# Eight single halves: another division of the weight splitting over ScalarE, VectorE and GpSimd in the expert stage

## The chip, the cores and the metric

One core of a Trainium2 chip. The metric is the device time of one execution in microseconds (us).

## The reference, cut to what matters

Linear attention, then a dense feed-forward layer (384 to 2048 to 384), then a mixture of 8 experts with one expert for each of the 1536 tokens. The change lies in the expert stage alone:

```
for e in range(8):                         # disp[e]: the tokens sent to expert e
    h[e] = maximum(disp[e] @ w1[e], 0)     # w1[e]: 384 x 1024
    y[e] = h[e] @ w2[e]                    # w2[e]: 1024 x 384
out[token] = gate_w[token] * y[expert of the token]
```

All of it is float32.

## The kernel before, in words

The attention and the dense layer take the first 300 us or so. In between, tokens are routed: their rows are scattered to a table in memory (`disp`), a region for each expert, and `counts` says how many there are. Then the experts run one after the other.

**Float32 in three products.** TensorE multiplies in a shorter format (`fp32r`). So each operand is split in a high part (a cast of the number) and a low part (the number less its high part), and high x high, high x low and low x high are summed. The weights of an expert are split on the chip too: four pieces `q` (two halves of `w1`, two of `w2`), each in two halves `x` of 128x768 numbers. `split_expert` (L667) does one half: a cast (L674 on ScalarE, L676 on VectorE), then a subtraction (L677). That makes eight casts and eight subtractions for each expert.

**One block.** `expert_block` (L758) computes 128 tokens of one expert. On TensorE: `hidden(0)` (nine matmuls, L775), five matmuls of `hidden(1)`, four transposes of the first half of the hidden layer (L784), the last four matmuls of `hidden(1)`, transposes of the next expert's rows (L658), three quarters of the first products with `w2` (L799), the second transposes, and the rest of the products. ScalarE does the two relus (L779) and the two casts of the transposed hidden layer (`hh`, L789); VectorE makes its low parts (`hl`, L790), and the result times the gate weight (`y`, L683). GpSimd scatters `y` to the output by an indirect DMA (L684, "put").

**Work beside a block.** `also(n)` (L765) stands at five places of a block and issues what the dictionary `beside` (L835 to L839) holds for it. In an expert's first block this is the splitting for the next expert. Before: place 0 (behind the matmuls of `hidden(0)`, ahead of the first relu): piece 0, cast and subtraction on VectorE. Place 1 (ahead of the first `hh`): piece 1, cast on ScalarE, subtraction on GpSimd. Place 2: transposes of the next expert's rows. Place 3 (behind the second relu, ahead of the second `hh`): piece 2, as piece 1. Place 4: the rows' own split (`d`, L663 and L664), then piece 3, cast on ScalarE, subtraction on VectorE. Each engine works in the order in which its instructions are issued.

**More blocks.** Up to three blocks, the second and third under a condition on the number of tokens (L846). With these inputs experts 0 to 3 have two blocks, expert 4 three, experts 5, 6 and 7 one (part of expert 0 was done earlier). Every engine reads the count itself (L1123) and branches.

**Loads.** SP's queue issues them in order. `load_expert(e + 2)` fetches the raw weights of the expert after the next (L392, L395), and waits until the same buffers' last splitting (expert e) is done. `load_rows(e)` (L639, its DMA on L644) fetches an expert's rows; there are three buffers, so the rows of e + 3 wait for the last put of expert e. Before, the loop at L1117 issues `load_rows(e + 3)` behind expert e, and so ahead of `load_expert(e + 3)`.

Of the kernel before, what the change touches and what calls it, by code (L numbers as in the profile page):

```python
# [23 lines left out]
def kernel(  # L24
# [16 lines left out]
    nc = tc.nc  # L41
# [4 lines left out]
    E = w_gate.shape[1]  # L46
# [337 lines left out]
    def load_expert(e, q):  # L384
        if q % 2 == 0:
            if e % 2 == 0:
                raws[("e", e)] = wpool.tile([P, 2 * PIECE], F32, tag="w", name=f"re{e}_{q}")
            else:
                raws[("e", e)] = late["p"].tile([P, 2 * PIECE], F32, tag=f"lraw{q}", name=f"re{e}_{q}")
        t = raws[("e", e)][:, (q % 2) * PIECE:(q % 2 + 1) * PIECE]  # L390
        if q < 2:
            nc.sync.dma_start(t.rearrange("p (c f) -> p c f", c=DC),  # L392
                              w1[e, :, q * HF:(q + 1) * HF].rearrange("(c p) f -> p c f", p=P))
        else:
            nc.sync.dma_start(t.rearrange("p (c d) -> p c d", d=DM),  # L395
                              w2[e, (q - 2) * HF:(q - 1) * HF, :].rearrange("(c p) d -> p c d", p=P))
        raws[("e", e, q)] = t
# [238 lines left out]
    def region(e):  # L636
        return (E - 1 - e) * STRIDE

    def load_rows(e):  # L639
        pool, tag = ((p1, "rows"), (late["p"], "lrows"), (late["p"], "erows"))[e % 3]  # L640
        t = pool.tile([P, SB, ROW], F32, tag=tag, name=f"drow{e}")
        base = region(e) + (P if e == 0 else 0)
        for b0, b1 in ((0, 1), (1, 2), (2, SB)) if e == 0 else ((0, SB),):
            nc.sync.dma_start(t[:, b0:b1], disp[base + b0 * P:base + b1 * P, :].rearrange("(b p) d -> p b d", p=P))  # L644
        dsp[e] = t

    def claim(e):

        dT[e] = [p2.tile([P, DC, STRIDE], F32R, tag=("xh", "xl")[x], name=f"d{x}_{e}") for x in range(2)]
        for q in range(NPIECE):  # L650
            wsl[("e", e, q)] = wpool.tile([P, 2 * PIECE], F32R, tag="w", name=f"we{e}_{q}")

    def prep(e, b):

        t = dsp[e]
        pt = bank(f"pd{e}_{b}", "acc")
        for c in range(DC):
            nc.tensor.transpose(pt[:, c * P:(c + 1) * P], t[:, b, c * P:(c + 1) * P], ident)  # L658
        src = pt[:, 0:DM].rearrange("p (c t) -> p c t", c=DC)
        hi = dT[e][0][:, :, b * P:(b + 1) * P]  # L660

        def g():
            nc.scalar.copy(hi, src)  # L663
            nc.vector.tensor_tensor(dT[e][1][:, :, b * P:(b + 1) * P], src, hi.bitcast(F32), ALU.subtract)  # L664
        return g

    def split_expert(e, q, x, he, le):  # L667
        src = raws[("e", e, q)]
        t = wsl[("e", e, q)]
        h = PIECE // 2  # L670
        sl = slice(x * h, (x + 1) * h)
        sl2 = slice(PIECE + x * h, PIECE + (x + 1) * h)
        if he is nc.scalar:
            nc.scalar.copy(t[:, sl], src[:, sl])  # L674
        else:
            he.tensor_copy(t[:, sl], src[:, sl])  # L676
        le.tensor_tensor(t[:, sl2], src[:, sl], t[:, sl].bitcast(F32), ALU.subtract)  # L677
# [147 lines left out]
    def expert(e, val):  # L825

        beside = {}
        if e + 1 < E:
            got = []

            def split(q, he, le):
                for x in range(2):
                    split_expert(e + 1, q, x, he, le)

            beside = {0: [lambda: split(0, nc.vector, nc.vector)],  # L835
                      1: [lambda: split(1, nc.scalar, nc.gpsimd)],
                      2: [lambda: got.extend(prep(e + 1, b) for b in range(2))],
                      3: [lambda: split(2, nc.scalar, nc.gpsimd)],
                      4: [lambda: [g() for g in got], lambda: split(3, nc.scalar, nc.vector)]}  # L839
        if e == 0:  # L840
            for g in [prep(0, b) for b in range(2)]:
                g()
        expert_block(e, 0, beside)

        def more(b):
            with tc.If(val > b * P):  # L846
                got = []
                expert_block(e, b, {2: [lambda: got.append(prep(e, b + 1))], 4: [lambda: got[0]()]} if b + 1 < SB else {})
                if b + 1 < SB:
                    more(b + 1)  # L850
        more(1)


    with tc.manual_schedule():
# [140 lines left out]
        for q in range(NW):  # L995
            for x in range(2):
# [9 lines left out]
                for n, p in enumerate(CONVERT.get(at, OTHERS)):  # L1006
                    g = at + p // 5
# [3 lines left out]
        for i in range(FRONT, NTILE):  # L1011
            blk = max(x for x in range(NBLK) if FIRST[x] <= i)
            sub = i - FIRST[blk]
            for f, then, at in PHASES:
                g = (blk - 1) * NFT + at[sub]
# [50 lines left out]
        g, n = NBLK * NFT - 1, SIZES[-1]  # L1066
# [50 lines left out]
        for e in range(E):  # L1117
            if e + 1 < E:
                claim(e + 1)
            if e + 2 < E:  # L1120
                for q in range(NPIECE):
                    load_expert(e + 2, q)
            val = nc.values_load(counts[0:1, e:e + 1], min_val=0, max_val=NT)  # L1123
            if e == 0:
                load_rows(2)
            expert(e, val)
            if e + 3 < E:
                load_rows(e + 3)


# [28 lines left out]
```

## Time and profile before

| | us |
|---|---|
| median of 3 runs | 471.08 (470.81 to 471.49) |
| the profiled execution | 470.56 |
| its span, first to last instruction | 468.8 |
| TensorE matmul busy | 437.5 (93%) |
| TensorE weight load busy | 383.7 (82%) |
| VectorE busy | 287.4 (61%) |
| ScalarE busy | 196.3 (42%) |
| GpSimd busy | 170.4 (36%) |

All times below are us from the start of the span. PE is TensorE, PEld its weight load, DVE VectorE, ACT ScalarE, POOL GpSimd, SP the queue that issues the loads; a q behind an engine's name is its sequencer. A line of a timeline has start, duration, engine, line of the kernel, operation, output<-input, the number of tokens of the matmul or the shape, the count, and in brackets the idle time just before it and what ended it. A line of windows has the stretch, its length, the busy time of PE, PEld, DVE, ACT and POOL with the number of their instructions, the clock granted to TensorE as a share of the full one, the DMA engines' busy share and the GB/s that they moved. The expert stage runs from about 316 to the end.

### The profile page before, as it was taken

The numbers are of one execution on the slowest core, as the hardware profiler recorded it, in microseconds if no ns is written. First come the engines' busy times: TensorE is split into PE (matmuls) and PEld (weight loads), VectorE is DVE, ScalarE is ACT, GpSimd is POOL, SyncE is SP. The second block draws the span as 40 slices with busy tenths as digits, with TensorE's granted clock in tenths as the row PEclk, the third lists the DMA queues.
The fourth block names the chain that finished last, engine by engine and source line by source line (L and its number), as shares of the span: only waits on it lengthen the run. The fifth ranks groups of instructions, "written<-read, shape, count | busy, mean of one in ns | idle before, by whom it ended". The sixth has DMA issues, their size and how long they took to land. (4 is left out here: it accounts for less than half of the span.)

```text
span 468.8 us, 7834 instructions
## 1 busy us (share of the span) xinstructions
PE 437.5 (93%) x3039; PEld 383.7 (82%) x3039; DVE 287.4 (61%) x477; ACT 196.3 (42%) x330; POOL 170.4 (36%) x145
## 2 busy tenths in 40 slices
PE   7977989699899999999999999999999999999975
PEld 6765778488788898989988889988888988888864
DVE  6898998999744354436334764346564556644771
ACT  1336644444444333323434444327264553624731
POOL 6845457464240232101200120036262543622760
PEclk9998999989999999999999999999999999999988
DMA  7999950559510208002600020039281835630900
GB/s 136 219 258 262 332 146 18 168 168 367 158 35 1 51 1 279 9 0 107 233 0 1 5 81 0 1 102 330 97 308 52 315 131 211 230 126 25 323 18 9
DMA packets 70603, 62.28 MB, mean 133 GB/s; under 512 B 41934, under 2 KB 58238, under 8 KB 70560
## 3 DMA queue, kind: packets, MB, share of 16 engines
q1 hardware_dynamic: 68832, 57.29, 39.8%
q0 software_dynamic: 1728, 4.40, 2.5%
q8 instruction: 28, 0.46, 0.4%
q14 instruction: 15, 0.12, 0.1%
HBM read 49.99 MB, written 12.62 MB: 134 GB/s over the span
## 5 line engine op out<-in xcount | busy, mean ns | idle before, releaser
L584 PE MATMUL acc<-wm,gh 128*128 128x384 f32 x384 | 100.9, 343 | 0.5 <-POOL wm L368 0.5
L599 PE MATMUL h<-xh,wm 128*128 128x512 f32 (+1 forms) x294 | 87.0, 405 | 3.8 <-DVE gl L622 3.8
L618 DVE SCALAR_TENSOR_TENSOR h<-ng,sign,h 128x512 f32<-128x512 f32 x48 | 36.1, 752 | 67.9 <-ACT ng L615 67.9
L584 PEld LDWEIGHTS acc<-wm,gh 128*128 128x128 f32 x384 | 68.8, 188 | 4.9 <-POOL wm L368 1.1
L775 PE MATMUL eh<-we,d 128*128 128x512 f32 x252 | 65.1, 403 | 4.3 <-PEq L846 4.3
L584 PE MATMUL acc<-wm,gl 128*128 128x384 f32 x192 | 64.9, 338 | 0.0
L599 PEld LDWEIGHTS h<-xh,wm 128*128 128x128 f32 x294 | 53.0, 191 | 13.4 <-issue 2.9
L677 POOL TENSOR_TENSOR we<-re,we 128x768 fp32r<-128x768 f32 x28 | 54.0, 1959 | 16.3 <-ACT we L674 16.2
L775 PEld LDWEIGHTS eh<-we,d 128*128 128x128 f32 x252 | 45.7, 188 | 15.1 <-issue 5.1
L615 ACT ACTIVATE ng<-h,slope 128x512 f32<-128x512 f32 x48 | 33.0, 688 | 57.0 <-PE h L599 57.0
L619 ACT CAST gh<-h 128x512 fp32r<-128x512 f32 x48 | 28.1, 586 | 63.7 <-DVE h L618 63.7
L799 PE MATMUL ey<-we,hh 128*128 128x384 f32 x224 | 49.0, 352 | 0.0
L522 POOL DMA_INDIRECT disp<-rows,sl x12 | 12.6, 1052 | 99.9 <-DVE run L543 64.4
L368 POOL TENSOR_TENSOR wm<-rm,wm 128x768 fp32r<-128x768 f32 x16 | 31.5, 1966 | 47.6 <-ACT wm L367 43.8
L790 DVE TENSOR_TENSOR hl<-pht,hh 128x512 fp32r<-128x512 f32 x28 | 19.3, 691 | 47.0 <-ACT hh L789 45.2
L677 DVE TENSOR_TENSOR we<-re,we 128x768 fp32r<-128x768 f32 x36 | 46.8, 1316 | 1.0 <-ACT we L674 0.3
L599 PE MATMUL h<-xl,wm 128*128 128x512 f32 (+1 forms) x147 | 42.9, 401 | 0.7 <-DVE xl L270 0.7
L622 DVE TENSOR_TENSOR gl<-h,gh 128x512 fp32r<-128x512 f32 x48 | 33.0, 687 | 15.6 <-ACT gh L619 15.6
L779 ACT ACTIVATE hs<-eh 128x512 f32<-128x512 f32 x28 | 16.8, 600 | 58.6 <-PE eh L775 58.6
L674 ACT CAST we<-re 128x768 fp32r<-128x768 f32 x50 | 39.6, 839 | 0.0
L799 PEld LDWEIGHTS ey<-we,hh 128*128 128x128 f32 x224 | 38.9, 193 | 0.4 <-ACT hh L789 0.4
L684 POOL DMA_INDIRECT out_dram<-y,drow x14 | 14.5, 1035 | 63.7 <-DVEq L846 38.6
(182 smaller groups left out, 659.2 us busy)
## 6 DMA issues: line engine op xcount, KB each, us to landing
re<-in_moe_w_dram SPq DMA_DIRECT2D x32, 768.0 KB, 8.5
rm<-in_moe_w_in_dram SPq DMA_DIRECT2D x8, 768.0 KB, 8.2
rm<-in_moe_w_out_dram SPq DMA_DIRECT2D x8, 768.0 KB, 6.6
disp<-rowss SPq DMA_DIRECT2D x1, 4825.0 KB, 17.3
drow<-disp SPq DMA_DIRECT2D x7, 579.0 KB, 4.2
out_dram<-rowss SPq DMA_DIRECT2D x1, 2304.0 KB, 22.6
kn<-in_k_dram SPq DMA_DIRECT2D x10, 192.0 KB, 4.4
rn<-in_r_dram SPq DMA_DIRECT2D x10, 192.0 KB, 4.8
```

What stands on the lines that cost most here:

```text
L368: eng.tensor_tensor(lo, low.bitcast(F32), hi.bitcast(F32), ALU.subtract)
L584: nc.tensor.matmul(accs[(blk, s)], gs[g][a][:, s * P:(s + 1) * P], wout[b][:, ft % 2, :], start=(ft == 0 and n == 0), stop=(ft == NFT - 1 ...
L599: nc.tensor.matmul(phs[g][:, cols[0]:cols[1]], win[a][:, c, o:o + P], xs[b][:, c, cols[0]:cols[1]], start=(n == 0), stop=(n == 3 * DC - 1))
L615: nc.scalar.activation(ng, ph, AF.Relu, scale=slope[:, ft:ft + 1])
L618: nc.vector.scalar_tensor_tensor(ph, ng, sign[:, ft:ft + 1], ph, op0=ALU.mult, op1=ALU.add)
L619: nc.scalar.copy(gh, ph)
L622: nc.vector.tensor_tensor(gl, ph, gh.bitcast(F32), ALU.subtract)
L674: nc.scalar.copy(t[:, sl], src[:, sl])
L677: le.tensor_tensor(t[:, sl2], src[:, sl], t[:, sl].bitcast(F32), ALU.subtract)
L775: nc.tensor.matmul(ph[q], d[x][:, c, :], ww[y][:, c, :], start=(n == 0), stop=(n == 3 * DC - 1))
L790: nc.vector.tensor_tensor(hl, pt, hh.bitcast(F32), ALU.subtract)
L799: nc.tensor.matmul(py, hT[q][x][:, c * P:(c + 1) * P], ww[y][:, c, :], start=(q == 0 and not low and c == 0 and y == 0), stop=(q == 1 and ...
```

## The change

Where the eight halves of the splitting stand in a block, and on which engine. All eight casts are on ScalarE. Subtractions: five on VectorE (V), three on GpSimd (G). And `load_rows(e + 2)` moves behind `load_expert(e + 2)`, ahead of expert e.

```
-            def split(q, he, le):
-                for x in range(2):
-                    split_expert(e + 1, q, x, he, le)
-
-            beside = {0: [lambda: split(0, nc.vector, nc.vector)],
-                      1: [lambda: split(1, nc.scalar, nc.gpsimd)],
+            def split(*what):
+
+                return [lambda q=q, x=x, le=le: split_expert(e + 1, q, x, nc.scalar, le) for q, x, le in what]
+
+            V, G = nc.vector, nc.gpsimd
+            beside = {0: split((0, 0, V), (0, 1, V)),
+                      1: split((1, 0, G)),
                       2: [lambda: got.extend(prep(e + 1, b) for b in range(2))],
-                      3: [lambda: split(2, nc.scalar, nc.gpsimd)],
-                      4: [lambda: [g() for g in got], lambda: split(3, nc.scalar, nc.vector)]}
+                      3: split((1, 1, V), (2, 0, G)),
+                      4: [lambda: [g() for g in got], *split((2, 1, V), (3, 0, V), (3, 1, G))]}
...
             if e + 2 < E:
                 for q in range(NPIECE):
                     load_expert(e + 2, q)
+                load_rows(e + 2)
             val = nc.values_load(counts[0:1, e:e + 1], min_val=0, max_val=NT)
-            if e == 0:
-                load_rows(2)
             expert(e, val)
-            if e + 3 < E:
-                load_rows(e + 3)
```

## Rows read from the trace of the kernel before

**Rows 1.** Windows by expert: 1, 5, 6 (columns: end of the profile section above).

```profile
337.50:358.00 20.50, 19.72 (x109) 17.55 (x109) 12.01 (x15) 10.15 (x17) 9.25 (x6) 1.00 0.58 203
...
428.00:438.20 10.20, 10.17 (x58) 8.88 (x56) 6.72 (x10) 7.41 (x12) 7.53 (x5) 1.00 0.55 189
438.20:453.50 15.30, 11.98 (x56) 10.42 (x56) 14.38 (x14) 7.41 (x12) 10.86 (x6) 0.89 0.40 141
```

**Rows 2.** Timeline of TensorE, experts 5, 6 and the start of 7.

```profile
428.07 3.44 PE L775 MATMUL eh<-we,d 128*128 128x512 f32 x14
431.35 0.60 PE L784 MATMUL pht<-ident,hs 128*128 128x128 f32 x4
...
435.92 1.55 PE L799 MATMUL ey<-we,hh 128*128 128x384 f32 x8
...
438.72 3.51 PE L775 MATMUL eh<-we,d 128*128 128x512 f32 x14 [0.55 <-PEq L846]
...
448.83 1.65 PE L799 MATMUL ey<-we,hl 128*128 128x384 f32 x4 [2.73 <-DVE hl L790]
...
453.98 3.51 PE L775 MATMUL eh<-we,d 128*128 128x512 f32 x14 [0.55 <-PEq L846]
```

**Rows 3.** Windows inside expert 6: TensorE's wait, and the stretch behind it (columns as rows 1).

```profile
445.90:448.80 2.90, 0.20 (x2) 0.00 (x0) 2.90 (x3) 2.73 (x5) 2.90 (x2) 1.00 0.01 3
448.80:452.30 3.50, 3.47 (x11) 3.48 (x12) 3.50 (x4) 0.00 (x0) 2.84 (x2) 0.51 0.02 5
```

**Rows 4.** Timeline of VectorE, experts 5 and 6.

```profile
428.92 0.56 DVE L676 CAST we<-re 128x768 fp32r<-128x768 f32 x1
429.52 0.96 DVE L677 TENSOR_TENSOR we<-re,we 128x768 fp32r<-128x768 f32 x1
...
437.29 3.48 DVE L677 TENSOR_TENSOR we<-re,we 128x768 fp32r<-128x768 f32 x2
440.69 0.61 DVE L683 TENSOR_SCALAR y<-ey,drow 128x384 f32<-128x384 f32 x1
442.01 0.56 DVE L676 CAST we<-re 128x768 fp32r<-128x768 f32 x1 [0.72 <-DMA re<-in_moe_w_dram]
...
443.48 2.20 DVE L676 CAST we<-re 128x768 fp32r<-128x768 f32 x1
445.72 2.45 DVE L677 TENSOR_TENSOR we<-re,we 128x768 fp32r<-128x768 f32 x1
448.09 1.28 DVE L790 TENSOR_TENSOR hl<-pht,hh 128x512 fp32r<-128x512 f32 x2
```

**Rows 5.** Timeline of GpSimd, experts 4 to 6.

```profile
403.27 7.97 POOL L677 TENSOR_TENSOR we<-re,we 128x768 fp32r<-128x768 f32 x4 [3.01 <-ACT we L674]
...
429.17 1.16 POOL L684 DMA_INDIRECT out_dram<-y,drow  x1 [8.29 <-DVE y L683]
431.83 7.24 POOL L677 TENSOR_TENSOR we<-re,we 128x768 fp32r<-128x768 f32 x4 [1.50 <-ACT we L674]
...
442.78 8.86 POOL L677 TENSOR_TENSOR we<-re,we 128x768 fp32r<-128x768 f32 x4
```

**Rows 6.** Timeline of SP's queue: rows and weights of expert 7.

```profile
432.09 0.37 SPq L644 DMA_DIRECT2D drow<-disp  x1
432.55 0.97 SPq L392 DMA_DIRECT2D re<-in_moe_w_dram  x2
```

**Rows 7.** The page's DMA issues: line, engine, count, KB each, us to landing.

```profile
re<-in_moe_w_dram SPq DMA_DIRECT2D x32, 768.0 KB, 8.5
```

**Rows 8.** Timeline of ScalarE, expert 5.

```profile
430.43 0.60 ACT L779 ACTIVATE hs<-eh 128x512 f32<-128x512 f32 x1 [4.71 <-PE eh L775]
...
435.12 0.59 ACT L789 CAST hh<-pht 128x512 fp32r<-128x512 f32 x1
...
436.34 1.59 ACT L674 CAST we<-re 128x768 fp32r<-128x768 f32 x2
```

**Rows 9.** Groups by line, 316 to 454: ScalarE's casts, busy and mean ns.

```profile
L674 ACT CAST we<-re 128x768 fp32r<-128x768 f32 x42 | 33.0, 840 | 0.0
```

## The prediction

> **What bounds the kernel now.** I read the windows by expert first, to see in which experts TensorE is not full. In expert 1 it is busy 19.72 of 20.50 us, and the missing 0.78 us is one gap at an expert's start, which the timeline puts down to TensorE's own sequencer at the branch; expert 5 is full, 10.17 of 10.20; expert 6 is not, 11.98 of 15.30 [rows 1]. Experts 0 and 2 to 4 look like expert 1. So in seven of eight experts nothing that the other engines do is on the path, and faster splitting is worth nothing there. Expert 6 is where time can be had: both have one block, yet from start to start expert 5 takes 438.72 - 428.07 = 10.65 us and expert 6 453.98 - 438.72 = 15.26 us, which is 4.61 us more [rows 2].
>
> Next the timeline of TensorE in expert 6: one wait of 2.73 us, ended by VectorE's `hl` [rows 2]. Behind it the granted clock is 0.51 for some 3.5 us, the lower of the two levels (1.2 against 2.4 GHz); ahead of it and in the wait it was 1.00 [rows 3]. Half speed for 3.5 us is some 1.75 us more, and 2.73 + 1.75 = 4.48, nearly all of the 4.61.
>
> Why `hl` was late stands in VectorE's and GpSimd's timelines [rows 4, 5]. Four things follow on one another. (1) In expert 5, VectorE's last two subtractions take 3.48 us where one alone takes 0.96: they meet GpSimd's run of four, which ends at 431.83 + 7.24 = 439.07. (2) So `y` of expert 5, queued behind, comes at 440.69, though TensorE began expert 6 at 438.72. (3) VectorE's first cast of expert 6 starts at 442.01, the last 0.72 us waiting for expert 7's weights: those loads were issued from 432.55, behind the rows [rows 6]; landing takes a median of 8.5 us [rows 7]. (4) Then the second cast takes 2.20 us and the subtraction 2.45 us, beside GpSimd's run from 442.78. `hl` is queued behind all that, at 448.09.
>
> **The change, part by part.**
>
> *Casts of piece 0, from VectorE to ScalarE.* VectorE loses two casts of 0.56 us an expert [rows 4], ScalarE gains two of 0.84 [rows 9]. They now stand ahead of the first relu in ScalarE's queue, and behind that relu wait TensorE's transposes. ScalarE is idle 4.71 us before that relu [rows 8], so two casts (some 1.6 us) have room. In expert 5 the relu starts at 430.43, ends at 431.03, and the transposes come at 431.35 [rows 2, 8]: 0.32 us to spare. The casts are late only if they start after 430.43 + 0.32 - 1.59 = 429.16, that is 1.09 us after TensorE's first matmul. How soon ScalarE may start, no row shows; VectorE's cast into the same buffer started at 428.92, 0.85 us after it, and not before its own `y` was done [rows 4]. Bounds: no delay, or, should ScalarE start as late as VectorE did in expert 6 (3.29 us after the first matmul), 2.2 us. I take none, as the cast of expert 5 is the nearest row, and ScalarE has no `y` to do first.
>
> *Piece 1.* One cast instead of two ahead of the first `hh`, so `hh` and `hl` come up to 0.5 us sooner: nothing on the path. The other half moves to place 3, in a pair of casts ahead of the second `hh`, as many as before, so that `hh` still ends at 435.12 + 0.59 = 435.71, 0.21 us before the products that need it [rows 2, 8]. Zero, with a small margin.
>
> *Place 4.* ScalarE does three casts instead of two. Two ended at 436.34 + 1.59 = 437.93 [rows 8]; a third ends at about 438.7. TensorE started expert 6 at 438.72, so a one-block expert just holds it; should TensorE's next bank wait for ScalarE's branch, 0 to 0.2 us at each of two starts (experts 6 and 7). I take 0.1 for both together. After that ScalarE branches, casts piece 0 of expert 7 from about 439.3 to 440.9, and the relu of expert 6 is due at 438.72 + 2.36 = 441.1. It fits.
>
> *Subtractions.* GpSimd has three instead of four: 3 x 1.81 = 5.4 us of 10.65 instead of 7.2 [rows 5]. They are apart now: in expert 5 after the casts at about 431.8, 435.1 and 438.7, with gaps between. VectorE has five instead of four and no casts: 5 x 0.96 = 4.8 against 2 x 0.56 + 4 x 0.96 = 5.0 us without meetings. I place VectorE's in those gaps: half (1,1) at 434.3 to 435.3; the last two at 437.3 to 439.2, when GpSimd is idle. `y` of expert 5 then starts at about 439.2 instead of 440.69. In expert 6, `hl` of the first half comes at about 443.3 and of the second at about 446.4; TensorE wants the first at about 445.9 (where it began to wait before [rows 3]). It wants the second behind eight products that in expert 5 end at 435.92 + 1.55 = 437.47, 9.40 us after its start [rows 2], so at about 448.1. Both are early. So the wait of 2.73 us goes, and with it the fall of the clock: 4.61 us off.
>
> A meeting still costs: the row of 3.48 us against 2 x 0.96 says up to 1.6 us on VectorE each time. The Trainium skill (SBUF — State Buffer, "SBUF: two separate sides") says that a VectorE operation with two SBUF inputs and a GpSimd operation exclude each other for a whole instruction. By that rule five subtractions on VectorE can be held up where only four could before; the rows agree that a meeting costs nearly a whole GpSimd instruction (1.6 against 1.81), which gives a rival below.
>
> *Loads.* The weights of e + 2 no longer stand behind rows that wait for the put of e - 1. For expert 7 the rows' wait ended at 432.09, 2.9 us after expert 4's last put at 429.17 [rows 5, 6]. What is left to wait for is the splitting of expert 5, in expert 4's first block, whose GpSimd part ended at 403.27 + 7.97 = 411.24 [rows 5]. So the loads go at about 412, land some 8 to 10 us later, and the wait of 0.72 us goes; it lies inside the chain above, so no further gain. The rows of expert 7 go at 432 as before and are wanted at 443: nothing. SP issues no instruction more. Where two blocks follow, the loads were early enough and nothing changes.
>
> **Sum.** The profiled execution took 470.56 with a span of 468.8. 470.56 - 4.61 + 0.1 = 466.05. The median shown is 0.52 above that execution; on it the forecast is 466.6 us.
>
> **Rivals.**
>
> *Meetings remain* (GpSimd and VectorE subtract at the same time, and `hl` of the second half is late). If GpSimd's first half starts 0.4 us later in expert 6, VectorE's half (1,1) waits a whole 1.81 us, ends near 447.8, and `hl` near 448.5, 0.5 us late. In expert 6 alone that leaves 467.1; in all seven first blocks 7 x 0.5 = 3.5, which is 470.1. For it: the third subtraction on GpSimd comes at the very end of a one-block expert. Against: 1.0 to 1.5 us of room in expert 5. Chance 0.10, likely at 467 to 469.
>
> *The weights are late all the same* (SP is held by something that the rows do not show). Then ScalarE's cast in expert 6 waits until 442.0, the relu behind it starts at 443.6 and ends at 444.2, and TensorE waits 2.1 us for its transposes; with a clock fall of 1.75 that is 3.9 of the 4.6 given back: 470.4. Against: the only long wait ahead of these loads is that of the rows. Chance 0.04. This would also be how "the change does nothing" looks.
>
> *ScalarE late at every first relu* (slower). If whatever frees the buffers lets the casts start only 3.29 us after the first matmul, as in expert 6 before, each of seven first blocks loses 2.2 us: 466.6 + 15.4 = 482.0. It decides from 1.09 us on; the time is above the old one by 0.2% when the casts start on average about 1.9 us after. For it: ScalarE gets the slower casts, and one late cast now blocks relus. Against: 4.71 us of idle time before the relu, and VectorE's start at 0.85. In a sentence of its own: the Trainium skill (ScalarE: Activation LUTs, "Rules for kernel authors") advises VectorE for simple elementwise work, and its 186 ns + 0.833 ns an element makes 826 ns for such a cast, an estimate that the 840 ns here agree with [rows 9]. By that rule, were every ScalarE cast on the path, 14 of them at 0.84 - 0.56 = 0.28 us dearer would take 3.9 us of the gain. Chance of this rival 0.04.
>
> **How the numbers follow.** Forecast 0.82, meetings 0.10, late weights 0.04, ScalarE late 0.04. About 0.2%, 0.9 us, is what a measurement can tell. Faster: the forecast, most of the meetings, 0.91; the same: the late weights and the far end of the meetings, 0.05; slower 0.04. The range: below, the forecast less 0.8 us (no 0.1 us at the starts and the spread of the runs, 0.4 us, with a little more gained from `y` coming earlier); above, up to the middle of the meetings, 2 us: 465.8 to 468.6.
>
> **What would show it.** Expert 6 takes 10.6 to 10.8 us from start to start, like expert 5; no wait for `hl`; granted clock 1.00 through all experts; `y` of expert 5 near 439.2; expert 7's weight loads near 412; first relu still 2.3 to 2.5 us after an expert's first matmul. It would be wrong if the windows showed TensorE below 19.7 us in a two-block expert, or a wait on the first relu anywhere.

## The result, and the profile after

The changed kernel takes 466.36 us (median of 6 runs, 465.58 to 467.54), the kernel before, measured beside it, 470.94: a ratio of 0.9908, 95% interval 0.9892 to 0.9925, so 0.75% to 1.1% faster. The forecast was 466.6, range 465.8 to 468.6. The profiled execution took 466.23 with a span of 464.5; the forecast for it was 466.05. The kernels of the later rounds below that come out like the change are 3.6 to 4.1 us under the kernel before measured beside them, so the 4.5 us here are a figure of this round and of the two traces.

The windows by expert, after (columns as [rows 1]; expert 1, expert 5, expert 6):

```profile
337.60:358.10 20.50, 19.72 (x109) 17.55 (x109) 9.83 (x14) 11.78 (x20) 7.75 (x5) 1.00 0.66 221
428.00:438.20 10.20, 10.20 (x58) 8.95 (x56) 6.49 (x9) 6.98 (x12) 5.35 (x3) 1.00 0.24 80
438.20:448.90 10.70, 10.11 (x57) 8.91 (x56) 7.74 (x11) 9.01 (x15) 7.38 (x4) 1.00 0.04 13
```

Expert 1 has the same 19.72 busy us of TensorE as in [rows 1], to the hundredth, although VectorE does 2.2 us less beside it and ScalarE 1.6 more: there the splitting was not on the path. Expert 6 has a granted clock of 1.00 instead of 0.89, and TensorE is busy 10.11 of 10.70 us.

The timeline of TensorE after: starts of experts 5, 6 and 7, and the products in expert 6 that had waited for `hl` in [rows 2]:

```profile
428.14 3.44 PE L775 MATMUL eh<-we,d 128*128 128x512 f32 x14
...
438.83 3.54 PE L775 MATMUL eh<-we,d 128*128 128x512 f32 x14 [0.59 <-ACTq L847]
...
446.07 0.86 PE L799 MATMUL ey<-we,hl 128*128 128x384 f32 x4
...
449.61 3.54 PE L775 MATMUL eh<-we,d 128*128 128x512 f32 x14 [0.59 <-ACTq L847]
```

From start to start expert 5 takes 10.69 us (10.65 before), expert 6 takes 449.61 - 438.83 = 10.78 (15.26 before). The 4.48 us less in expert 6 are all of the gain between the two traces: the spans differ by 4.3, and the rest is tenths (expert 5 starts 0.07 later than before, and from expert 7's start to the end it is 14.9 instead of 14.8). The wait and the slow products are gone; the gap at an expert's start is 0.59 instead of 0.55 and is put down to ScalarE's branch; ScalarE now works up to the end of the block.

VectorE, after, from the end of expert 5 (against [rows 4]):

```profile
439.08 0.61 DVE L683 TENSOR_SCALAR y<-ey,drow 128x384 f32<-128x384 f32 x1
440.28 2.28 DVE L677 TENSOR_TENSOR we<-re,we 128x768 fp32r<-128x768 f32 x2 [0.59 <-ACT we L674]
443.47 0.69 DVE L790 TENSOR_TENSOR hl<-pht,hh 128x512 fp32r<-128x512 f32 x1 [0.91 <-ACT hh L789]
...
446.58 0.69 DVE L790 TENSOR_TENSOR hl<-pht,hh 128x512 fp32r<-128x512 f32 x1 [0.37 <-ACT hh L789]
```

`y` starts 1.6 us sooner, and `hl` at 443.47 instead of 448.09. Before each `hl` VectorE is now idle and waits for ScalarE's `hh`: its own queue no longer decides. One pair of subtractions still takes 2.28 us, where a pair alone takes 1.82: GpSimd's third one of expert 5 (the last line below) runs until 440.87. GpSimd's three subtractions of expert 5 stand apart, where [rows 5] have a run of four:

```profile
431.90 1.83 POOL L677 TENSOR_TENSOR we<-re,we 128x768 fp32r<-128x768 f32 x1 [1.10 <-ACT we L674]
435.18 1.95 POOL L677 TENSOR_TENSOR we<-re,we 128x768 fp32r<-128x768 f32 x1 [1.45 <-ACT we L674]
438.81 2.06 POOL L677 TENSOR_TENSOR we<-re,we 128x768 fp32r<-128x768 f32 x1 [1.68 <-ACTq L847]
```

ScalarE, after: casts of piece 0 beside expert 5 and beside expert 6, and expert 6's first relu:

```profile
425.76 1.57 ACT L674 CAST we<-re 128x768 fp32r<-128x768 f32 x2
...
439.26 1.57 ACT L674 CAST we<-re 128x768 fp32r<-128x768 f32 x2 [0.52 <-DVE we L677]
441.29 0.60 ACT L779 ACTIVATE hs<-eh 128x512 f32<-128x512 f32 x1 [0.47 <-PE eh L775]
```

Both pairs are over before the relu is due; those of expert 5 start 2.4 us ahead of TensorE's first matmul. SP's queue, after: expert 7's weights (two pieces of `w1`, two of `w2`) and, behind them, its rows:

```profile
406.69 0.90 SPq L392 DMA_DIRECT2D re<-in_moe_w_dram  x2
412.12 0.92 SPq L395 DMA_DIRECT2D re<-in_moe_w_dram  x2
432.54 0.37 SPq L644 DMA_DIRECT2D drow<-disp  x1
```

### The profile page after: what moved, and what is told of

Read it like the earlier page. It is cut to its first block, busy times and chain, and to the rows that moved or that the text cites. A ratio compares the mean times of both kernels' runs of the same rounds, so it can differ in the third digit from the quotient of the medians.

```text
span 464.5 us, 7861 instructions
## 1 busy us (share of the span) xinstructions
PE 437.4 (94%) x3039; PEld 385.1 (83%) x3039; DVE 271.0 (58%) x470; ACT 208.2 (45%) x344; POOL 157.7 (34%) x138
## 5 line engine op out<-in xcount | busy, mean ns | idle before, releaser
L584 PE MATMUL acc<-wm,gh 128*128 128x384 f32 x384 | 102.0, 347 | 0.5 <-POOL wm L368 0.5
L584 PEld LDWEIGHTS acc<-wm,gh 128*128 128x128 f32 x384 | 69.9, 191 | 4.7 <-POOL wm L368 0.8
L674 ACT CAST we<-re 128x768 fp32r<-128x768 f32 x64 | 50.6, 839 | 9.6 <-DMA re<-in_moe_w_dram 6.8
L677 POOL TENSOR_TENSOR we<-re,we 128x768 fp32r<-128x768 f32 x21 | 40.6, 1932 | 38.5 <-ACT we L674 32.2
L677 DVE TENSOR_TENSOR we<-re,we 128x768 fp32r<-128x768 f32 x43 | 40.3, 965 | 11.9 <-ACT we L674 8.9
L799 PEld LDWEIGHTS ey<-we,hh 128*128 128x128 f32 x224 | 37.8, 189 | 0.3 <-ACT hh L789 0.3
L584 PEld LDWEIGHTS acc<-wm,gl 128*128 128x128 f32 x192 | 36.6, 191 | 0.0
L599 PEld LDWEIGHTS h<-xl,wm 128*128 128x128 f32 x147 | 27.7, 191 | 7.0 <-DVE xl L270 0.3
```

Of the source, the lines that this page charges most:

```text
L584: nc.tensor.matmul(accs[(blk, s)], gs[g][a][:, s * P:(s + 1) * P], wout[b][:, ft % 2, :], start=(ft == 0 and n == 0), stop=(ft == NFT - 1 ...
L599: nc.tensor.matmul(phs[g][:, cols[0]:cols[1]], win[a][:, c, o:o + P], xs[b][:, c, cols[0]:cols[1]], start=(n == 0), stop=(n == 3 * DC - 1))
L799: nc.tensor.matmul(py, hT[q][x][:, c * P:(c + 1) * P], ww[y][:, c, :], start=(q == 0 and not low and c == 0 and y == 0), stop=(q == 1 and ...
```

## Experiments

The change has three parts: the order of the loads, the casts, and the places and engines of the subtractions. The question was which of them brings the 4.5 us. One number orders the kernels of the table: how long after TensorE's first matmul of expert 6 the first `hl` starts. TensorE wants the result 446.07 - 438.83 = 7.24 us after that matmul and `hl` takes 0.69, so a start at 6.55 is in time. The totals expected below were reckoned from the 471.08 us of the first measurement; beside the experiments the kernel before took 469.88 to 470.35, so totals are best compared as ratios.

| kernel | `hl` starts, us into expert 6 | expert 6, start to start | ratio to before, 95% interval |
|---|---|---|---|
| before | 9.37 | 15.26 | 1 |
| loads alone | 9.34 | 15.25 | 1.0006 (0.9992 to 1.002) |
| one word: casts on ScalarE | 6.66 | 10.99 | 0.9925 (0.9899 to 0.9952) |
| casts on ScalarE, early loads | 6.63 | 10.97 | 0.9904 (0.9881 to 0.9927) |
| subtractions apart, casts on VectorE | 6.43 | 10.80 | 0.9912 (0.9894 to 0.9929) |
| all subtractions on VectorE | 5.28 | 10.78 | 0.9925 (0.9908 to 0.9942) |
| the change without early loads | 4.63 | 10.77 | 0.9916 (0.9894 to 0.9938) |
| the change | 4.64 | 10.78 | 0.9908 (0.9892 to 0.9925) |

**Loads alone.** The kernel before with

```
+                load_rows(e + 2)
...
-            if e == 0:
-                load_rows(2)
...
-            if e + 3 < E:
-                load_rows(e + 3)
```

> The kernel before with the order of the loads alone changed. Theory (in expert 6 VectorE is late because its queue is long, and the weights that it waits for 0.72 us come only as late as its own branch ends): the weight loads of expert 7 move from 432.5 to about 412, VectorE's first cast of expert 6 moves from 442.01 to about 441.9 and no further, the cast and the subtraction behind it still take over 2 us beside GpSimd, TensorE still waits 2.5 to 2.8 us for hl, the granted clock still falls; expert 6 takes 15.0 to 15.3 us from start to start, total 470.5 to 471.3. Rival (late weights are the cause): no wait in expert 6, about 466.5.

470.31 us, ratio 1.0006: no gain. Its weights were issued at 406.01 and 411.19. VectorE and TensorE in its expert 6:

```profile
441.05 0.56 DVE L676 CAST we<-re 128x768 fp32r<-128x768 f32 x1 [0.69 <-DVEq L846]
...
442.52 2.21 DVE L676 CAST we<-re 128x768 fp32r<-128x768 f32 x1
...
447.13 1.27 DVE L790 TENSOR_TENSOR hl<-pht,hh 128x512 fp32r<-128x512 f32 x2
```

```profile
437.79 3.51 PE L775 MATMUL eh<-we,d 128*128 128x512 f32 x14 [0.55 <-PEq L846]
...
447.86 1.19 PE L799 MATMUL ey<-we,hl 128*128 128x384 f32 x4 [2.70 <-DVE hl L790]
...
453.04 3.27 PE L775 MATMUL eh<-we,d 128*128 128x512 f32 x13 [0.55 <-PEq L846]
```

The idle time ahead of VectorE's first cast is 0.69 us and now bears the name of VectorE's own branch. Before, 0.72 us at the same place bore the name of the DMA [rows 4]. The name went; the time stayed. The trace of the kernel before has a sign of it too, the landing of the two pieces of `w1` for expert 7 (the view by source line, 430 to 436):

```profile
DMA to landing us min/median/max: 5.6/6.9/8.1
```

Issued at 432.55 and about 433.0, both had landed by 433.0 + 8.1 = 441.1, and VectorE's idle time began only at the end of `y`, 440.69 + 0.61 = 441.30.

**The change without its early loads.** The changed kernel with the old lines of the loads.

> The changed kernel with the old order of the loads. Theory (the new division needs the early loads, as ScalarE's first cast of expert 6 now stands ahead of the first relu): that cast waits for the weights until about 442.0, the first relu of expert 6 ends at about 444.2 instead of 441.9, TensorE waits some 2.1 us for its transposes, expert 6 takes 12.9 us from start to start, or 14.6 if the clock falls; total 468.5 to 470.4. Rival (the division of the work is all, the loads add nothing): expert 6 takes 10.8 us, total 466.4.

The rival held: 466.24, ratio 0.9916, the same as the whole change. The step that fell was when the weights arrive. SP's queue, the landing of the two pieces of `w1` (the same view), and ScalarE:

```profile
432.75 0.96 SPq L392 DMA_DIRECT2D re<-in_moe_w_dram  x2
```

```profile
DMA to landing us min/median/max: 6.6/7.3/8.1
```

```profile
439.41 1.57 ACT L674 CAST we<-re 128x768 fp32r<-128x768 f32 x2 [0.96 <-DVE y L683]
441.02 0.60 ACT L779 ACTIVATE hs<-eh 128x512 f32<-128x512 f32 x1
```

Issued at 432.75, the first piece lands 6.6 us later, at about 439.35 (the 8.1 would put it behind the start of the casts that read it); the casts start at 439.41 and end just as the relu is due. The name on that wait is `y`, but in the change the same casts start at 439.26 while `y` runs until 439.69, so they don't wait for `y`; that they wait for the piece is read from the times. My 442.0 had come from the 0.72 us named after the DMA, the name that the run before this one shows to be wrong. So with the old order the weights come just in time, and the early loads add room, with no speed to be seen.

**Old subtractions.** The kernel before with the early loads and

```
-            beside = {0: [lambda: split(0, nc.vector, nc.vector)],
+            beside = {0: [lambda: split(0, nc.scalar, nc.vector)],
```

> Both the early loads and all casts on ScalarE, but pieces and subtractions where and on which engine they were before (four on GpSimd, four on VectorE). Theory (taking the two casts off VectorE is enough to bring hl in time but for a few tenths): VectorE's last two subtractions of expert 5 still take about 3.5 us and y comes at about 440.7; in expert 6 the subtractions run at 441.9 and 444.6, hl at about 445.6 to 446.2 against 445.9 wanted, a wait of up to 0.4 us; expert 6 takes 10.8 to 11.2 us, total 466.4 to 467.0. Rival (the meetings of VectorE and GpSimd are the cause, whoever casts): a wait of 1 us or more for hl in expert 6, total 467.5 to 470.

465.80, ratio 0.9904; expert 6 (from 438.41 to 449.38) takes 10.97 us. VectorE:

```profile
441.61 3.51 DVE L677 TENSOR_TENSOR we<-re,we 128x768 fp32r<-128x768 f32 x2 [0.62 <-ACT hs L779]
445.04 0.68 DVE L790 TENSOR_TENSOR hl<-pht,hh 128x512 fp32r<-128x512 f32 x1
```

VectorE's two subtractions in expert 6 still take 3.51 us beside GpSimd, and `hl` comes at 6.63 us, 0.1 behind the limit.

**One word.** The same edit without the early loads: in the whole kernel, `nc.vector` becomes `nc.scalar` in one place.

> The kernel before with one word changed: the casts of piece 0 on ScalarE; subtractions and loads as before. Theory (the two casts of piece 0 in VectorE's queue, with the meeting that one of them has with GpSimd, are the 2.7 us by which hl is late): VectorE's two subtractions of expert 6 still take about 3.5 us, hl comes at about 445 to 446, expert 6 takes 10.8 to 11.1 us, total 465.8 to 466.6, the same as the changed kernel. Rival (early loads or fewer subtractions on GpSimd are needed as well): 468 to 471.

466.64, ratio 0.9925; expert 6 (from 438.84 to 449.83) takes 10.99 us. VectorE and TensorE in expert 6:

```profile
442.09 3.48 DVE L677 TENSOR_TENSOR we<-re,we 128x768 fp32r<-128x768 f32 x2 [0.69 <-DMA re<-in_moe_w_dram]
445.50 0.68 DVE L790 TENSOR_TENSOR hl<-pht,hh 128x512 fp32r<-128x512 f32 x1
```

```profile
446.23 0.96 PE L799 MATMUL ey<-we,hl 128*128 128x384 f32 x4
```

From VectorE's start on the splitting to `hl` it is 445.50 - 442.09 = 3.41 us, against 448.09 - 442.01 = 6.08 in [rows 4]. The difference, 2.67, is nearly the whole wait of 2.73 us: two casts of 0.56, and the 1.6 us that the second of them lost beside GpSimd (2.20 against 0.56). `y` is as late as before (440.80). The idle time of 0.69 us bears the DMA's name here as well, although ScalarE had cast that very piece from 438.67 on: the name is wrong again.

**Subtractions apart, casts on VectorE.** The changed kernel with the old loads and

```
-... split_expert(e + 1, q, x, nc.scalar, le) for q, x, le in what]
+... split_expert(e + 1, q, x, V if q == 0 else nc.scalar, le) for q, x, le in what]
```

> The kernel before with the changed kernel's places and subtractions (five on VectorE, three on GpSimd, apart), but the two casts of piece 0 still on VectorE, and the old order of the loads. Theory (each of the two reliefs is enough: apart from GpSimd's run, y of expert 5 comes at about 439 and VectorE's queue in expert 6 ends in time): hl of the first half in expert 6 at about 446.1, wanted at 446.0; a wait of up to 0.3 us; expert 6 takes 10.7 to 11.1 us, total 466.0 to 466.9. Rival (the casts on VectorE are what makes hl late, wherever the subtractions stand): a wait above 1 us in expert 6, total above 467.5.

466.44, ratio 0.9912; expert 6 (from 440.06 to 450.86 in this execution) takes 10.80 us. VectorE:

```profile
441.54 0.98 DVE L676 CAST we<-re 128x768 fp32r<-128x768 f32 x1 [0.62 <-DVEq L847]
...
444.01 2.56 DVE L677 TENSOR_TENSOR we<-re,we 128x768 fp32r<-128x768 f32 x1
446.49 0.68 DVE L790 TENSOR_TENSOR hl<-pht,hh 128x512 fp32r<-128x512 f32 x1
```

One full meeting remains (2.56 us for a subtraction of 0.96) and the end of another (0.98 for a cast of 0.56), but VectorE starts on the splitting 1.48 us into the expert, as `y` is early, instead of 3.29. Of the 2.94 us by which `hl` is sooner that is 1.81; the other 1.13 are the splitting itself, 446.49 - 441.54 = 4.95 us instead of 6.08, with fewer meetings in expert 6 too. The early `y` by itself would leave `hl` at 9.37 - 1.81 = 7.56 us, 1.0 us late (worked out, not run). So either part of the change, the casts on ScalarE or the new places of the subtractions, brings `hl` to the limit, and their gains don't add.

**All subtractions on VectorE.** The changed kernel with `V, G = nc.vector, nc.vector`.

> The changed kernel with all eight subtractions on VectorE, none on GpSimd. Theory (GpSimd is not needed; VectorE has room for 8 x 0.96 us once the casts are gone and nothing meets it): y of expert 5 at about 441, VectorE's first subtraction of expert 6 at about 442, hl of the first half at about 445.4 (wanted at 446.1) and of the second at about 448.0 (wanted at 448.1); no wait or one under 0.3 us; expert 6 takes 10.7 to 11.0 us, total 466.0 to 466.8. Rival (three halves on GpSimd are needed): a wait of 0.5 to 2 us for hl in expert 6, total 467 to 469.

466.75, ratio 0.9925: GpSimd is not needed for the gain either. There is no wait for `hl`, and expert 6 (from 438.72 to 449.50) takes 10.78 us. VectorE:

```profile
441.38 2.69 DVE L677 TENSOR_TENSOR we<-re,we 128x768 fp32r<-128x768 f32 x3 [0.60 <-DVEq L847]
444.00 0.68 DVE L790 TENSOR_TENSOR hl<-pht,hh 128x512 fp32r<-128x512 f32 x1
```

Three subtractions in a row take VectorE 2.7 us, as it has nobody to meet; `hl` comes 1.4 us sooner than expected.

**Four casts ahead of the relu.** The changed kernel with

```
-            beside = {0: split((0, 0, V), (0, 1, V)),
-                      1: split((1, 0, G)),
+            beside = {0: split((0, 0, V), (0, 1, V), (1, 0, None), (1, 1, None)),
+                      1: low(1, 0, G),
...
-                      3: split((1, 1, V), (2, 0, G)),
+                      3: low(1, 1, V) + split((2, 0, G)),
```

where `None` leaves the subtraction to its old place, and `low` is that subtraction alone.

> The changed kernel with the four casts of pieces 0 and 1 all ahead of the first relu (two more than in the change). Theory (the relu has 0.32 us to spare and is pushed only where ScalarE cannot start early): in experts 1 to 5 ScalarE starts the casts 0.66 us or more ahead of TensorE's first matmul and four still end before the relu is due, no wait; in expert 0 the casts end about 0.9 us after the relu was due, a wait of about 0.6 us; in expert 6 the relu comes 1.0 us later, a wait of about 0.7 us; clock 1.00; total 467.4 to 467.9. Rival (ScalarE is late at every first relu): a wait in each of seven blocks, 0.7 to 1.2 us each, total 471 to 475.

467.68, ratio 0.9939 (0.9920 to 0.9958): 1.3 us above the change by the medians, as the theory has it, though the interval meets that of the change (0.9892 to 0.9925). ScalarE and TensorE in expert 6:

```profile
439.71 3.17 ACT L674 CAST we<-re 128x768 fp32r<-128x768 f32 x4 [0.58 <-DVE we L677]
442.79 0.59 ACT L779 ACTIVATE hs<-eh 128x512 f32<-128x512 f32 x1
```

```profile
443.43 0.66 PE L784 MATMUL pht<-ident,hs 128*128 128x128 f32 x4 [0.66 <-ACT hs L779]
```

The relu is 1.1 us later than in the change, TensorE waits 0.66 for it, and expert 6 takes 11.65 us instead of 10.78; expert 0 has a wait of 0.44, experts 1 to 5 none. So the mechanism of the rival "ScalarE late at every first relu" is real, but it needs more casts than the change puts there, and an expert that ScalarE enters late.

**The clock.** In the kernel before, part of the 4.6 us was put to the fall of TensorE's clock behind the wait. To see it alone, the wait was filled:

```
+        if e == 6 and b == 0:
+            keep_warm("warm_6", "att", 12, d[0][:, 0, :], exp_w(e, 0)[0][:, 0, :])
         second(0, True)
```

> The kernel before, with 12 matmuls of 512 columns put into TensorE's queue in expert 6 where it waits for hl; their results are used by nothing. Theory (the granted clock falls because TensorE stands idle 2.73 us, and the fall costs some 1.7 us by itself): the wait is filled for about 2.8 us, hl comes as late as before, the granted clock stays at 1.00 behind it, expert 6 takes 13.4 to 13.7 us from start to start instead of 15.26, total lower by 1.4 to 1.8 us, ratio 0.996 to 0.997. Rival (the clock falls for another reason, or the fall costs nothing): 15.2 us or more, ratio 1.000 or above.

This missed its aim: 473.88, ratio 1.0069. The timeline of TensorE shows why:

```profile
448.95 4.60 PE L756 MATMUL warm<-we,d 128*128 128x512 f32 x12 [2.73 <-DVE hl L790]
```

The 12 matmuls waited for `hl` themselves: their PSUM bank was that of the transposed hidden layer, which `hl` reads. They filled nothing and ran at the lower clock (0.52 granted from 449.0 to 452.5). A second try took a bank of the other pair (`"h"` for `"att"`).

> The kernel before, again with 12 unused matmuls of 512 columns in expert 6 ahead of the products that wait for hl, now into a PSUM bank of the other pair, whose reader (the first relu) is long done, so that they need not wait for hl themselves. Theory (the granted clock falls because TensorE stands idle 2.73 us, and the fall alone costs some 1.7 us): the 12 run at 0.23 us each from about 446.0 to 448.8, hl comes as late as before, clock 1.00 behind it; expert 6 takes 13.4 to 13.8 us from start to start instead of 15.26; ratio 0.996 to 0.997. Rival (the clock falls all the same, or the fall costs nothing): 15.2 us or more, ratio 1.000 or above.

469.23, ratio 0.998 (0.9963 to 0.9996). TensorE, and the windows of the wait and of the stretch behind it (columns as [rows 1]):

```profile
446.21 2.97 PE L756 MATMUL warm<-we,d 128*128 128x512 f32 x12
449.12 0.97 PE L799 MATMUL ey<-we,hl 128*128 128x384 f32 x4
```

```profile
446.00:449.00 3.00, 3.00 (x15) 2.28 (x13) 3.00 (x3) 2.84 (x6) 3.00 (x2) 1.00 0.01 3
449.00:452.50 3.50, 3.21 (x17) 2.77 (x16) 3.50 (x5) 0.00 (x0) 2.98 (x2) 1.00 0.02 5
```

`hl` is as late as before (9.39 us into the expert), but the clock stays at 1.00 (0.51 in [rows 3]), and expert 6 takes 13.76 us instead of 15.26. So of the 4.48 us some 1.5 belong to the clock and 3.0 to the wait in these traces. The runs give 0.2% for the filling, less than the 0.3 to 0.4% expected, with an interval of 0.04% to 0.37%, 0.2 to 1.7 us: it includes the 1.5 of the trace, but does not fix it. The three shortest executions of the kernel before in that round (468.16 to 468.57) have a mean clock of 0.990 over the whole span, eight of the other ten 0.979 to 0.987. So the clock may not have fallen behind the wait in each execution, and the filling may have had nothing to save in some. That is not shown: no trace of such an execution was kept, and the first 100 us move the mean clock too (0.95 to 0.98 in the traces).

## Why the prediction was right, and where it was not

**The place and the size.** TensorE full in all experts but one, a wait for `hl` in expert 6 and a slow stretch behind it: right, and in the traces the only place where time came from. Forecast 4.61 us off, measured 4.48. The split into 2.73 of waiting and 1.75 of clock is 3.0 and 1.5 by the filled wait. The total stood on 471.08 for the kernel before, which came out at 470.94 beside the change and a little lower in every later round.

**The late `hl`, links (1), (2) and (4).** Right in kind: VectorE and GpSimd meeting at the end of expert 5, the late `y`, the cast of 2.20 us. What the prediction did not see is that either of two reliefs is enough: the two casts off VectorE, with the one meeting of theirs (2.7 us), or the subtractions apart, which bring `y` forward and leave fewer meetings in expert 6 (2.9 us). It added everything up in one chain; the experiments show a limit at 6.55 us that each relief reaches by itself to within 0.1 us (6.66, 6.43), with hardly anything left for the other. So the time alone, as forecast, could not show which part had brought it: one word would have given the same within what the runs can tell.

**Link (3), the weights.** Wrong: the 0.72 us were not a wait for weights. With the weights issued over 20 us earlier they were still 0.69, and bore the name of VectorE's own branch, as 0.60 and 0.62 us do at this place in two other runs. It cost the sum nothing, as I had counted the loads for no further gain; that was luck, for I took the 0.72 us for a wait that would go, inside the chain, and it stayed. But it set the price of the second rival (late weights, 470.4): run as an experiment, that came out at 466.24. Its step "ScalarE's cast in expert 6 waits until 442.0" failed; the cast started at 439.41, as the first piece lands after 6.6 us (the 8.5 of [rows 7] is the median of all 32 loads).

**Casts on ScalarE.** The bounds were 0 and 2.2 us, taken as 0; measured 0, with starts 2.4 us ahead of TensorE (expert 5) and 0.43 us after it (expert 6). The point from which it decides, 1.09 us for two casts, was tested with four: in expert 6 they start 0.48 us after the first matmul, two casts (1.6 us) more is as if two had started at 2.1, so 1.0 us too late; measured 0.66 of waiting, and 0.87 in the length of the expert. The point is about right, 0.1 to 0.3 us too early.

**Place 4 and the branch.** Forecast 0.1 us for two starts; measured 0.04 each, 0.59 against 0.55. No row had given the size. With two casts there (the kernel with one word changed) the gaps are 0.55 and 0.56.

**Subtractions.** `y` of expert 5 at 439.2 in the forecast, 439.08 measured; `hl` at 443.3 and 446.4, measured 443.47 and 446.58. The rival "meetings remain" did not come: VectorE's 43 subtractions last 965 ns in the mean (36 of 1316 before), and the one meeting left in expert 6, 0.5 us in the pair of 2.28, was off the path. The Trainium skill (SBUF — State Buffer, "SBUF: two separate sides") has VectorE's operations with two SBUF inputs, and its copies and casts when they run in a two-port mode, exclude GpSimd's for a whole instruction, and gives ScalarE ports of its own. By that rule moving casts to ScalarE takes them out of the contest; the runs agree: ScalarE's casts last 0.84 us in the mean before and after, while VectorE's lasted 0.56 alone and 2.20 beside GpSimd.

**Loads.** Forecast near 412; `w2` went at 412.12, `w1` at 406.69; its buffers are split first. Worth nothing here.

## What to carry to other kernels

Look for the one stage where the bounding engine waits, and ask how late its input is and against what limit; several reliefs of one wait don't add up, and the smallest (here one word) may bring nearly all of it (expert 6 in 10.99 us instead of 15.26, against 10.78 with the whole change). The name that a profile gives to a short idle time can be that of something that had nothing to do with it; take the suspect away and see whether the time goes too. A short wait of TensorE can cost more than its length, so price the slow stretch behind it as well.

## What the runs showed of the hardware that was not expected

In these traces the fall of the clock came behind the idle time, not in it: 1.00 during the 2.73 us of waiting, 0.51 in the 3.5 us after, when TensorE is at work again [rows 3]; idle gaps of 0.8 us at four experts' starts and of 0.66 in the run with four casts left it at 1.00 (windows of 316 to 428 before, and of 439.2 to 450.9 in that run). With the wait filled it stayed at 1.00. And filling an idle stretch with useless matmuls made this kernel faster only where they could start: with a PSUM bank whose reader was the late instruction itself they cost 3.5 us (473.88 against 470.35), with another bank they saved about one (469.23 against 470.15).
